# Where the second network enters a fused attention and two-network kernel, and how its weight conversions are ranked

## The chip, the cores and the metric

One core of a Trainium2 chip. The metric is device time of one execution in microseconds (us); lower is better. The engines are named as in the profile: PE (TensorE, matmuls), DVE (VectorE), ACT (ScalarE), POOL (GpSimd) and SP (SyncE, which here only issues transfers).

## The reference

Channel attention over 6016 tokens of 256 channels, then two feed-forward networks, token by token:

```python
qn = q / (norm(q, axis=tokens) + 1e-6);  kn = k / (norm(k, axis=tokens) + 1e-6)
a = softmax(kn.T @ qn / tau)                      # 256 x 256
x = v @ a
h = x @ w_in                                      # first network, 2048 wide
g = where(h >= 1, h, where(h <= -1, 0, (h + 1)**2 / 4))
x = g @ w_out
xn = x / sqrt(mean(x*x, axis=-1) + 1e-6) * rms_g  # second network, 1536 wide
s = xn @ w_gate
out = (s * sigmoid(s) * (xn @ w_val)) @ w_out2
```

All weights come as 64-bit floats, q, k and v as 32-bit.

## The kernel before

**Tiles.** The tokens are cut into 12 tiles t of 512 (the last has 384). Each product is done with operands split into a high and a low part of a matmul type of lower precision (hi by an ACT copy, lo by a DVE subtraction, `split`), and three matmuls per product: high-high, high-low, low-high. A **block** ("1", t, f) of the first network is 128 of the 2048 inner columns: `emit_A`, six matmuls into a PSUM tile h (line L555); `start_g`, two ACT passes and one DVE pass that make g (L564 to L566), the last of which frees the PSUM tile; `finish_g`, the split into gh and gl; and `emit_B`, six matmuls into y (L587), BLAG = 3 blocks later. A block ("2", t, f) of the second network is 128 of 1536 columns: twelve matmuls into gp and vp (L658), Silu and a product (L668, L669), a split into uh and ul, and two such blocks later `emit_D`, six matmuls into the output o (L702; L692 for the last tile).

**Between the networks.** `norm(t)` copies y out of PSUM into an SBUF tile x, makes the sum of squares sa, splits it into sh and sl, adds over partitions by two matmuls into ms (L615, L616), takes a power on POOL, scales x and splits it into xh and xl. It is a generator: each `work(1)` runs it to its next `yield`. `prep_v` does the like for the next tile of v (transposed into vt, split into vh and vl).

**Weights.** The attention matrix is multiplied into w_in once, in four pieces (`product_a`, into w1_ps, evicted into w1h and w1l). Each 64-bit weight piece is loaded into a tile `wide` and made into a high and a low 32-bit part by `narrow`: per piece four or five DVE steps and three or four ACT steps (L203 to L230, and the last subtraction in L120). 34 pieces: eight of w_in, eight of w_out, and 18 of the second network. `pump` advances at most two of them by a step each; `may_W2` holds back the second network's until item W2_FROM of the order.

**The order.** A list `order` of blocks is traced one after the other; behind each, `work` and `pump`. In it the blocks of tiles 0 and 1 are interleaved, then eight blocks of tile 2 (ALONE), then first and second network mixed, 24 blocks of the second remaining at the end. The framework's scheduler then sets each engine's order by its own estimate, by readiness and by rank (traced earlier ranks first); it may split a group of six matmuls. `issue_after(ins)` keeps the traced instructions of an engine behind `ins` on that engine; with `gates` it holds the conversions' steps behind tile 1's last split, until item GATED. `in_order` fixes an engine's order as traced.

**Buffers.** Four PSUM tiles (tag mm) for h, gp, vp, ms and w1_ps in turn, two (yo) for y and o. In SBUF four tmp tiles (g, u, vt, sa, sb and the output tiles ob), three each for gh and gl (sh and sl too), and eight opp tiles (vh, vl, xh, xl).

Of the kernel before, what the change touches and what calls it, by code (L numbers as in the profile page):

```python
# [27 lines left out]
BORROW = (0, 15)  # L28
LENT = 1
# [17 lines left out]
def tile_channel_attention_two_ffn(  # L47
# [270 lines left out]
    jobs += early_jobs[:EARLY]  # L318
    late_wi = early_jobs[EARLY:]

    for at_job, job in zip((0, 3, 4, 7, 8), late_wi):
        later.insert(at_job, job)
    w2 = {}
    for g in range(F2 // TOK):
# [108 lines left out]
        return sub_hi(v_op[t][1][:, c, :], vt[t][c], v_op[t][0][:, c, :])  # L433

    at = []

    def product_a(g):

        h, l = wi.pop(g)
        got = []  # L440
        for b in range(NC):
            ah, al = at[b]
            ps = mm_tile(f"w1_ps{g}_{b}")
            terms = [(ah, w, c) for c in range(NC) for w in (h, l)]
            terms += [(al, h, c) for c in range(NC)]
            for i, (x, w, c) in enumerate(terms):
                nc.tensor.matmul(  # L447
                    ps, x[:, c * P:(c + 1) * P], w[:, c, :],
                    start=(i == 0), stop=(i == len(terms) - 1),
                )  # L450
            got.append(ps)

        def evict(b):
            sl = slice(g * TOK, (g + 1) * TOK)
            hi, lo = w1h[:, b, sl], w1l[:, b, sl]
            nc.scalar.activation(out=hi, in_=got[b], func=AF.Copy, scale=rs[b])
            nc.vector.scalar_tensor_tensor(
                out=lo, in0=got[b], scalar=rs[b], in1=hi.bitcast(F32),
                op0=ALU.mult, op1=ALU.subtract,
            )  # L460

        return evict

# [80 lines left out]
    last_A = [None]  # L544
    g_op = {}
    g_f32 = {}

    def emit_A(t, f):
        _, n = tiles[t]
        vh, vl = v_op[t]  # L550
        ps = mm_tile(f"h{t}_{f}")
        terms = [(w1h, x, c) for c in range(NC) for x in (vh, vl)]
        terms += [(w1l, vh, c) for c in range(NC)]
        for i, (w, x, c) in enumerate(terms):
            last_A[0] = nc.tensor.matmul(  # L555
                ps[:, :n], w[:, c, f * P:(f + 1) * P], x[:, c, :n],
                start=(i == 0), stop=(i == len(terms) - 1),
            )
        return ps

    def start_g(t, f, ps):
        _, n = tiles[t]
        r = tmp_tile(f"g{t}_{f}")
        nc.scalar.activation(out=r[:, :n], in_=ps[:, :n], func=AF.Relu, bias=0.5, scale=0.5)  # L564
        nc.scalar.activation(out=r[:, :n], in_=r[:, :n], func=AF.Square)  # L565
        nc.vector.scalar_tensor_tensor(  # L566
            out=r[:, :n], in0=ps[:, :n], scalar=1.0, in1=r[:, :n], op0=ALU.max, op1=ALU.min
        )
        g_f32[t, f] = r

    def finish_g(t, f):
# [20 lines left out]

    x_op = {}

    def norm(t):
        _, n = tiles[t]
        y = y_ps.pop(t)
        nb = n // 32
        x = big_tile(f"x{t}", "x")
        nc.scalar.activation(out=x[:, 0, :n], in_=y[:, 0, :n], func=AF.Copy)  # L600
        nc.vector.tensor_copy(out=x[:, 1, :n], in_=y[:, 1, :n])
# [14 lines left out]
        nc.tensor.matmul(ps[:, :n], ones_r, sl[:, :n], start=False, stop=True)  # L616
        nc.vector.transpose(out=s1[:, :n], in_=ps[:, :n])
        m = const.tile([P, 16], F32, tag="m", name=f"m{t}")
        nc.gpsimd.tensor_scalar(
# [8 lines left out]
            in_=m[:, :nb].unsqueeze(2).to_broadcast([P, nb, 32]),  # L628
        )
        nc.vector.transpose(out=s1[:, :n], in_=s0[:, :n])  # L630
        for c in range(NC):
# [6 lines left out]
        xl = opp.tile([P, NC, TOK], F32R, tag="op", name=f"xl{t}")  # L638
        for c in range(NC):
            split(xh[:, c, :n], xl[:, c, :n], x[:, c, :n])  # L640
        x_op[t] = (xh, xl)


# [93 lines left out]
    order = [block for _, block in sorted(at_block)]  # L737

    second = [("2", t, f) for t in range(NT) for f in range(NF2)]
    done = 0  # L740
    for t in range(2, NT):
        first = ALONE if t == 2 else 0
        n = NF2 - HELD if t == 2 else NF2 + HELD if t == 3 else NF2
        base = done
        for f in range(NF1):
            order.append(("1", t, f))
            while done < base + n * (f + 1 - first) // (NF1 - first):
                order.append(second[done])
                done += 1
    order += [("B",)] * BLAG  # L750
    order += second[done:]

    tasks = []
    n_norms = [0]
# [12 lines left out]
    def finish_all_g():  # L767
        for key in list(g_f32):
            finish_g(*key)

    def step1(t, f):
        if t == 0 and f in W1_AT:
            make_w1(W1_AT.index(f) + 1)
        ps = emit_A(t, f)
        m1.append((t, f))
        finish_all_g()
        start_g(t, f, ps)
        if len(m1) > BLAG:
            next_B()

    def next_B():
        t, f = m1.pop(0)
        if (t, f) in g_f32:
            finish_all_g()
        if t == 0:
            require(("wo", f // 2))
        emit_B(t, f)
        if f == NF1 - 1:
            n_norms[0] += 1
            tasks.insert(n_norms[0] - 1, norm(t))  # L790

    def step2(t, f):
        if t == 0:
# [14 lines left out]
            store(t)  # L808

    jobs.extend(later)  # L810
    for i, it in enumerate(order):
        if it[0] == "1":
            _, t, f = it
            if t > 0 and f == 0 and t + 1 < NT:
                load_v(t + 1)
            if t > 0 and f == 8 and t + 1 < NT:
                tasks.append(prep_v(t + 1))
            if t == 2 and f >= 8:
                work(1)
            while t not in v_op:  # L820
                work(1)
            step1(t, f)
        elif it[0] == "2":
            while it[1] not in x_op:
                work(1)
            step2(*it[1:])
        else:
            next_B()
        work(1)
        pump()  # L830
        if i % 3 == 0:
            pump()
        if i == GATED:
            gates.clear()
        may_W2[0] |= i >= W2_FROM
    finish_u(*m2[-1])
    did_D(*m2[-2])
    did_D(*m2[-1])
# [35 lines left out]
```

## Time and profile before

| | us |
|---|---|
| median of 3 runs | 1187.37 (1185.89 to 1188.77) |
| the profiled execution | 1187.01 |
| its span in the profile | 1185.1 |
| PE busy | 1161.7 (98%) |
| DVE busy | 664.9 (56%) |
| ACT busy | 648.0 (55%) |
| POOL busy | 68.5 (6%) |

The profiled execution is 1.9 us longer than its span. Busy shares are averages over the span; the slices in [rows 1] are 29.6 us each. The matmuls are pipelined: a matmul of 512 columns is recorded with about 0.39 us, and the next starts about 0.226 us after it, so a busy PE is not PE at its peak, and the number of matmuls in a stretch says more.

### The profile page before, as it was taken

Reading aid. Unit: us, or ns where it says so; the run is one execution under the profiler, and the core shown is the slowest. Engines: PE = TensorE matmul, PEld = TensorE weight load, DVE = VectorE, ACT = ScalarE, POOL = GpSimd, SP = SyncE. Lnnn points to the kernel's source line nnn. Section 1 sums busy time; section 2 is a strip of 40 time slices with the busy share of each in tenths; the row PEclk is TensorE's granted clock in tenths of the full one; section 3 lists DMA queues with packets and bytes.
Section 4 is the critical chain, followed back from the end, with each engine's and each line's share of the span. In section 5 each row is a group of like instructions: output and inputs, shape, how many; then the busy total and the mean of one; then the engine's idle time right before and its main releaser. Section 6 shows DMA issues by size and latency. Waiting matters only on the chain.

```text
span 1185.1 us, 13913 instructions
## 1 busy us (share of the span) xinstructions
PE 1161.7 (98%) x5202; PEld 969.6 (82%) x5202; DVE 664.9 (56%) x1034; ACT 648.0 (55%) x1092; POOL 68.5 (6%) x54
## 2 busy tenths in 40 slices
PE   8889997999999999999999999999999999999998
PEld 6768885888888888888888888888888888888888
DVE  5899999664434644644644643653653654544433
ACT  6689988554445544644644554554555554444332
POOL 0000011010002001001101101100100100100000
PEclk9989998999999999999999999999999999999999
DMA  9923432101101101101010010110100100100110
GB/s 347 248 88 107 124 107 72 18 1 19 18 1 19 19 1 18 17 3 19 1 19 11 8 19 1 19 18 1 18 14 1 19 1 1 19 1 1 19 18 14
DMA packets 107747, 43.36 MB, mean 37 GB/s; under 512 B 97568, under 2 KB 97952, under 8 KB 107680
## 3 DMA queue, kind: packets, MB, share of 16 engines
q1 hardware_dynamic: 107680, 42.48, 14.3%
q8 instruction: 40, 0.66, 0.2%
q14 instruction: 27, 0.22, 0.1%
HBM read 36.31 MB, written 6.16 MB: 36 GB/s over the span
## 4 chain that ended last, share of the span: by engine, by line
PE 90%; DVE 5%; DMA 2%; ACT 1%; issue 1%; SPq 0%; DVEq 0%; ACTq 0%
PE y L587 20%; PE h L555 20%; PE gp L658 16%; PE vp L658 16%; PE o L702 15%; DVE acc L378 1%; PE o L692 1%; PE w_ps L447 1%; DMA qk<-in_k_dram 1%; DMA qk<-in_q_dram 1%; DVE g L566 1%; DVE wide L222 1%; DVE wide L214 1%; DVE gl L120 0%; DMA wide<-in_moe_w_val_dram 0%
## 5 line engine op out<-in xcount | busy, mean ns | idle before, releaser
L566 DVE SCALAR_TENSOR_TENSOR g<-h,g 128x512 f32<-128x512 f32 (+1 forms) x192 | 129.8, 677 | 188.9 <-ACT g L565 188.6
L123 ACT ACTIVATE uh<-u 128x512 fp32r<-128x512 f32 (+1 forms) x144 | 89.8, 624 | 202.2 <-PE o L702 147.1
L564 ACT ACTIVATE g<-h 128x512 f32<-128x512 f32 (+1 forms) x192 | 112.7, 588 | 130.9 <-PE h L555 126.6
L669 DVE TENSOR_TENSOR u<-u,vp 128x512 f32<-128x512 f32 (+1 forms) x144 | 97.2, 675 | 128.8 <-PE vp L658 120.4
L123 ACT ACTIVATE gh<-g 128x512 fp32r<-128x512 f32 (+1 forms) x192 | 118.9, 621 | 82.7 <-DVE g L566 81.2
L555 PE MATMUL h<-vh,w1h 128*128 128x512 f32 (+1 forms) x384 | 149.8, 390 | 3.1 <-DVE g L566 3.1
L555 PE MATMUL h<-vl,w1h 128*128 128x512 f32 (+1 forms) x384 | 149.5, 389 | 0.0
L120 DVE TENSOR_TENSOR gl<-g,gh 128x512 fp32r<-128x512 f32 (+1 forms) x168 | 113.5, 677 | 64.0 <-ACT gh L123 61.3
L587 PE MATMUL y<-gh,woh 128*128 128x512 f32 (+1 forms) x384 | 148.9, 388 | 0.1
L120 DVE TENSOR_TENSOR ul<-u,uh 128x512 fp32r<-128x512 f32 (+1 forms) x144 | 97.6, 677 | 91.4 <-ACT uh L123 91.4
L587 PE MATMUL y<-gh,wol 128*128 128x512 f32 (+1 forms) x384 | 148.3, 386 | 0.0
L565 ACT ACTIVATE g<-g 128x512 f32<-128x512 f32 (+1 forms) x192 | 119.6, 623 | 5.0
L587 PE MATMUL y<-gl,woh 128*128 128x512 f32 (+1 forms) x384 | 118.3, 386 | 0.6 <-DVE gl L120 0.6
L555 PE MATMUL h<-vh,w1l 128*128 128x512 f32 (+1 forms) x384 | 118.5, 389 | 0.0
L668 ACT ACTIVATE u<-gp 128x512 f32<-128x512 f32 (+1 forms) x144 | 84.9, 590 | 49.5 <-PE gp L658 32.4
L658 PE MATMUL gp<-xh,wgh 128*128 128x512 f32 (+1 forms) x288 | 111.0, 385 | 0.0
L658 PE MATMUL vp<-xh,wvh 128*128 128x512 f32 (+1 forms) x288 | 111.0, 385 | 0.0
L658 PE MATMUL gp<-xh,wgl 128*128 128x512 f32 (+1 forms) x288 | 110.9, 385 | 0.0
L658 PE MATMUL vp<-xh,wvl 128*128 128x512 f32 (+1 forms) x288 | 110.8, 385 | 0.0
L702 PE MATMUL o<-uh,wdh 128*128 128x512 f32 x264 | 102.8, 390 | 0.0
L702 PE MATMUL o<-uh,wdl 128*128 128x512 f32 x264 | 102.8, 389 | 0.0
L555 PEld LDWEIGHTS h<-vh,w1h 128*128 128x128 f32 x384 | 72.9, 190 | 19.0 <-DVE g L566 4.4
(121 smaller groups left out, 1751.4 us busy)
## 6 DMA issues: line engine op xcount, KB each, us to landing
wide<-in_moe_w_out_dram SPq DMA_DIRECT2D x14, 512.0 KB, 3.9
vin<-in_v_dram SPq DMA_DIRECT2D x88, 64.0 KB, 2.5
out_dram<-ob SPq DMA_DIRECT2D x88, 64.0 KB, 2.0
qk<-in_q_dram SPq DMA_DIRECT2D x9, 512.0 KB, 10.2
qk<-in_k_dram SPq DMA_DIRECT2D x9, 512.0 KB, 10.2
wide<-in_moe_w_in_dram SPq DMA_DIRECT2D x8, 512.0 KB, 6.9
wide<-in_moe_w_gate_dram SPq DMA_DIRECT2D x6, 512.0 KB, 3.5
wide<-in_moe_w_val_dram SPq DMA_DIRECT2D x6, 512.0 KB, 3.7
```

What stands on the lines that cost most here:

```text
L120: return eng.tensor_tensor(out=dst_lo, in0=src, in1=hi.bitcast(F32), op=ALU.subtract)
L123: nc.scalar.activation(out=dst_hi, in_=src, func=AF.Copy)
L214: nc.vector.scalar_tensor_tensor(out=low, in0=high, scalar=0x80000000, in1=low, op0=ALU.bitwise_and, op1=ALU.bitwise_or,)
L555: last_A[0] = nc.tensor.matmul(ps[:, :n], w[:, c, f * P:(f + 1) * P], x[:, c, :n], start=(i == 0), stop=(i == len(terms) - 1),)
L564: nc.scalar.activation(out=r[:, :n], in_=ps[:, :n], func=AF.Relu, bias=0.5, scale=0.5)
L565: nc.scalar.activation(out=r[:, :n], in_=r[:, :n], func=AF.Square)
L566: nc.vector.scalar_tensor_tensor(out=r[:, :n], in0=ps[:, :n], scalar=1.0, in1=r[:, :n], op0=ALU.max, op1=ALU.min)
L587: nc.tensor.matmul(y_ps[t][:, c, :n], w[:, f, c * P:(c + 1) * P], x[:, :n], start=(f == 0 and w is woh and x is gh), stop=(f == NF1 - 1 an ...
L658: nc.tensor.matmul(ps[:, :n], w[:, c, f * P:(f + 1) * P], x[:, c, :n], start=(i == 0), stop=(i == len(terms) - 1),)
L668: nc.scalar.activation(out=u[:, :n], in_=ps[0][:, :n], func=AF.Silu)
L669: nc.vector.tensor_tensor(out=u[:, :n], in0=u[:, :n], in1=ps[1][:, :n], op=ALU.mult)
L702: nc.tensor.matmul(o_ps[t][:, c, :n], w[:, f, c * P:(c + 1) * P], x[:, :n], start=(f == 0 and w is wdh and x is uh), stop=(f == NF2 - 1 an ...
```

## The change

- The second network's blocks begin 60 blocks behind the first network's beginning (FIRST_ALONE), then 12 for 16; 45 of them remain at the end.
- `take_y` copies y out of PSUM at the next block of the first network, into an opp tile (nine now); `norm` starts 14 items ahead of the tile's first block of the second network, has three yields ahead of its two matmuls for each tile, and three yields more behind them.
- The blocks and the `work` stages are traced in `high_priority`, so the conversions (`pump`) rank behind them. They are held behind the last block's square and DVE pass (`paced`), until item 50.
- The pieces of w_in come in another order, and their products with the attention matrix stand behind items 5, 13 and 21, with the evictions behind the next item.
- From item 32 PE keeps the traced order.

```diff
-PAIR = (1.5, 19.0)
-GATED = 6
-W2_FROM = 28
-ALONE = 8
-HELD = 8
+PAIR = (1.5, 16.5)
+W2_FROM = 20
+FIRST_ALONE = 60
+NORM_LEAD = 14
+PE_FROM = 32
+GATED = 50
+PACE = 1
+AHEAD_OF = 300
 BLAG = 3
-W1_AT = (2, 6, 10)
+W1_AT = (5, 13, 21)
...
-    opp = ctx.enter_context(tc.tile_pool(name="opp", bufs=8))
+    opp = ctx.enter_context(tc.tile_pool(name="opp", bufs=9))
...
-    for at_job, job in zip((0, 3, 4, 7, 8), late_wi):
+    for at_job, job in zip((1, 4, 5, 8, 9), late_wi):
...
     def make_w1(g):
         require(*[("wi", g, c) for c in range(NC)])
-
-        with tc.issue_after(last_A[0].ins):
-            evict = product_a(g)
-        for b in range(NC):
-            evict(b)
+        evict = product_a(g)
+        evicts.extend((evict, b) for b in range(NC))
...
+        if t < 3:
+            paced.append((on_act.ins, on_dve.ins))
         g_f32[t, f] = r
...
-    def norm(t):
+    def take_y(t):
         _, n = tiles[t]
         y = y_ps.pop(t)
-        nb = n // 32
-        x = big_tile(f"x{t}", "x")
+        x = opp.tile([P, NC, TOK], F32, tag="op", name=f"x{t}")
         nc.scalar.activation(out=x[:, 0, :n], in_=y[:, 0, :n], func=AF.Copy)
         nc.vector.tensor_copy(out=x[:, 1, :n], in_=y[:, 1, :n])
-        yield
+        y_sb[t] = x
+
+    def norm(t):
...
+        x = y_sb.pop(t)
...
-        for _ in range(3 if t < 2 else 1):
+        for _ in range(3):
             yield
         ps = mm_tile(f"ms{t}")
...
+    first += [("1", t, f) for t in range(2, NT) for f in range(NF1)]
...
+    for i, block in enumerate(first):
+        order.append(block)
+        while done * NF1 < (i + 1 - FIRST_ALONE) * NF2:
+            order.append(second[done])
+            done += 1
     order += [("B",)] * BLAG
     order += second[done:]
+    norm_at = {max(0, order.index(("2", t, 0)) - NORM_LEAD): t for t in range(NT)}
...
     for i, it in enumerate(order):
+        if i == PE_FROM:
+            ordered.enter_context(in_order(ENG.PE))
+        if i in norm_at:
+            n_norms[0] += 1
+            tasks.insert(n_norms[0] - 1, norm(norm_at[i]))
...
-            step1(t, f)
+            with tc.high_priority(AHEAD_OF):
+                step1(t, f)
+            if i in W1_AT:
+                make_w1(W1_AT.index(i) + 1)
+            else:
+                while evicts:
+                    evict, b = evicts.pop(0)
+                    evict(b)
...
-        work(1)
+        with tc.high_priority(AHEAD_OF):
+            work(1)
         pump()
         if i % 3 == 0:
             pump()
+        if len(paced) > PACE:
+            gates[:] = paced.pop(0)
         if i == GATED:
             gates.clear()
```

What moves, on DVE where the first blocks begin (behind the two splits vl of tile 1; g0_0 is the g of block (0, 0), `wide` a weight piece in conversion). Before:

```order
L120 TENSOR_TENSOR vl1_368<-vt1_1_370,vh1_367 128x512
L203 TENSOR_SCALAR wide_459<-wide_459 128x512
L210 TENSOR_SCALAR wide_459<-wide_459 128x512
L203 TENSOR_SCALAR wide_461<-wide_461 128x512
L210 TENSOR_SCALAR wide_461<-wide_461 128x512
L203 TENSOR_SCALAR wide_467<-wide_467 128x512
L203 TENSOR_SCALAR wide_457<-wide_457 128x512
L214 SCALAR_TENSOR_TENSOR wide_459<-wide_459 128x512
L566 SCALAR_TENSOR_TENSOR g0_0_453<-h0_0_446,g0_0_453 128x512
```

And now:

```order
L123 TENSOR_TENSOR vl1_368<-vt1_1_370,vh1_367 128x512
L206 TENSOR_SCALAR wide_459<-wide_459 128x512
L206 TENSOR_SCALAR wide_457<-wide_457 128x512
L213 TENSOR_SCALAR wide_457<-wide_457 128x512
L217 SCALAR_TENSOR_TENSOR wide_459<-wide_459 128x512
L217 SCALAR_TENSOR_TENSOR wide_457<-wide_457 128x512
L572 SCALAR_TENSOR_TENSOR g0_0_453<-h0_0_446,g0_0_453 128x512
L572 SCALAR_TENSOR_TENSOR g0_1_482<-h0_1_471,g0_1_482 128x512
```

Five conversion steps instead of seven stand ahead of the first g, and the g of block (0, 1) follows it at once.

On DVE where it makes gl of block (2, 8) (sb1, sa1 and sl1 belong to the norm of tile 1; wgl, wvl and wdl are low parts of the second network's weights). Before:

```order
L606 TENSOR_TENSOR sb1_1568<-x1_1554 128x512
L222 SCALAR_TENSOR_TENSOR wide_1929<-wide_1929 128x512
L120 TENSOR_TENSOR wvl_443<-wide_1895,wvh_442 128x512
L566 SCALAR_TENSOR_TENSOR g2_8_1583<-h2_8_1572,g2_8_1583 128x512
L607 TENSOR_TENSOR sa1_1567<-sa1_1567,sb1_1568 128x512
L566 SCALAR_TENSOR_TENSOR g2_9_1610<-h2_9_1599,g2_9_1610 128x512
L120 TENSOR_TENSOR wdl_445<-wide_1929,wdh_444 128x512
L203 TENSOR_SCALAR wide_1997<-wide_1997 128x512
L120 TENSOR_TENSOR sl1_1594<-sa1_1567,sh1_1593 128x512
L120 TENSOR_TENSOR gl2_8_1607<-g2_8_1583,gh2_8_1606 128x512
```

And now:

```order
L225 SCALAR_TENSOR_TENSOR wide_1508<-wide_1508 128x512
L217 SCALAR_TENSOR_TENSOR wide_1515<-wide_1515 128x512
L123 TENSOR_TENSOR gl2_7_1610<-g2_7_1579,gh2_7_1609 128x512
L206 TENSOR_SCALAR wide_1591<-wide_1591 128x512
L572 SCALAR_TENSOR_TENSOR g2_9_1637<-h2_9_1626,g2_9_1637 128x512
L123 TENSOR_TENSOR gl2_8_1634<-g2_8_1613,gh2_8_1633 128x512
L123 TENSOR_TENSOR wdl_445<-wide_1508,wdh_444 128x512
L217 SCALAR_TENSOR_TENSOR wide_1591<-wide_1591 128x512
L225 SCALAR_TENSOR_TENSOR wide_1515<-wide_1515 128x512
L123 TENSOR_TENSOR gl2_9_1657<-g2_9_1637,gh2_9_1656 128x512
```

The norm of tile 1 has left this place, and a conversion step or two stand between one g or gl and the next.

On PE at the first matmul of a norm's sum (ms1 before, ms0 now). Before:

```order
L615 MATMUL ms1_1643<-sh1_1593,ones_r_86 128x512
L555 MATMUL h2_10_1660<-vh2_1027,w1h_82 128x512
L555 MATMUL h2_10_1660<-vl2_1028,w1h_82 128x512
L555 MATMUL h2_10_1660<-vh2_1027,w1h_82 128x512
L555 MATMUL h2_10_1660<-vl2_1028,w1h_82 128x512
L555 MATMUL h2_10_1660<-vh2_1027,w1l_83 128x512 x2
L587 MATMUL y2_1422<-gh2_8_1606,woh_438 128x512
L587 MATMUL y2_1422<-gh2_8_1606,wol_439 128x512
L587 MATMUL y2_1422<-gh2_8_1606,woh_438 128x512
L587 MATMUL y2_1422<-gh2_8_1606,wol_439 128x512
L616 MATMUL ms1_1643<-sl1_1594,ones_r_86 128x512
```

And now:

```order
L595 MATMUL y3_1911<-gh3_0_1858,woh_438 128x512
L595 MATMUL y3_1911<-gh3_0_1858,wol_439 128x512
L595 MATMUL y3_1911<-gl3_0_1859,woh_438 128x512 x2
L629 MATMUL ms0_1918<-sh0_1844,ones_r_86 128x512
L630 MATMUL ms0_1918<-sl0_1845,ones_r_86 128x512
L561 MATMUL h3_4_1921<-vh3_1447,w1h_82 128x512
L561 MATMUL h3_4_1921<-vl3_1448,w1h_82 128x512
```

Before, ten matmuls stand between the two of ms, and a group of y is split by the second; now they follow each other, behind the whole of a block's second product.

## Rows read from the trace of the kernel before

**Rows 1.** The page: busy us, share and instructions; busy tenths in 40 slices; granted clock.

```profile
PE 1161.7 (98%) x5202; PEld 969.6 (82%) x5202; DVE 664.9 (56%) x1034; ACT 648.0 (55%) x1092; POOL 68.5 (6%) x54
...
PE   8889997999999999999999999999999999999998
...
DVE  5899999664434644644644643653653654544433
...
PEclk9989998999999999999999999999999999999999
```

**Rows 2.** Busy time by stretch: from:to, length, each engine busy (starts), PEclk, DMA share, GB/s.

```profile
62.00:67.30 5.30, 1.51 (x6) 0.59 (x4) 5.30 (x12) 5.30 (x11) 0.00 (x0) 0.93 0.22 91
67.30:74.60 7.30, 6.81 (x16) 4.99 (x17) 7.30 (x13) 7.27 (x15) 0.00 (x0) 0.58 0.00 0
74.60:178.00 103.40, 103.27 (x453) 84.63 (x453) 99.99 (x177) 92.02 (x168) 3.22 (x2) 1.00 0.39 112
178.00:192.00 14.00, 12.34 (x51) 8.91 (x49) 14.00 (x26) 13.04 (x25) 0.00 (x0) 1.00 0.39 114
192.00:204.00 12.00, 7.22 (x19) 5.44 (x20) 10.91 (x20) 9.86 (x17) 0.00 (x0) 0.72 0.15 44
57.60:204.00 146.40, 135.55 (x560) 107.69 (x559) 141.66 (x251) 130.84 (x236) 3.22 (x2) 0.95 0.36 104
204.00:300.00 96.00, 96.00 (x425) 79.48 (x424) 55.51 (x86) 49.77 (x84) 7.10 (x4) 1.00 0.07 12
...
300.00:400.00 100.00, 100.00 (x442) 82.81 (x441) 46.41 (x71) 47.59 (x78) 6.97 (x5) 1.00 0.07 11
1000.00:1100.00 100.00, 100.00 (x483) 88.02 (x482) 47.47 (x78) 47.10 (x87) 6.16 (x5) 1.00 0.04 6
```

**Rows 3.** Timeline of PE, 62 to 75 us: start, length, instruction, [idle before it, releaser].

```profile
64.57 0.50 PE L447 MATMUL w_ps<-w1h,ah 128*128 128x512 f32 x1 [1.79 <-DVE g L566]
...
67.31 0.80 PE L555 MATMUL h<-vh,w1h 128*128 128x512 f32 x1 [2.01 <-DVE g L566]
...
74.08 0.72 PE L447 MATMUL w_ps<-w1h,ah 128*128 128x512 f32 x2 [0.49 <-ACT w1h L228]
...
74.64 0.39 PE L587 MATMUL y<-gh,wol 128*128 128x512 f32 x1
```

**Rows 4.** Timeline of PE, 178 to 204 us.

```profile
180.14 0.50 PE L555 MATMUL h<-vh,w1h 128*128 128x512 f32 x1 [1.05 <-DVE g L566]
...
192.08 0.73 PE L587 MATMUL y<-gl,woh 128*128 128x512 f32 x2 [0.59 <-DVE gl L120]
...
197.52 0.79 PE L615 MATMUL ms<-sh,ones_r 128*128 128x512 f32 x1 [4.70 <-ACT sh L123]
...
203.41 0.40 PE L587 MATMUL y<-gh,woh 128*128 128x512 f32 x1
```

**Rows 5.** Timeline of DVE, 59 to 65 us.

```profile
59.82 1.47 DVE L120 TENSOR_TENSOR vl<-vt,vh 128x512 fp32r<-128x512 f32 x2
61.21 0.42 DVE L203 TENSOR_SCALAR wide<-wide 128x512 f32<-128x512 f32 x1
61.54 0.42 DVE L210 TENSOR_SCALAR wide<-wide 128x512 uint32<-128x512 uint32 x1
...
63.23 0.69 DVE L214 SCALAR_TENSOR_TENSOR wide<-wide 128x512 uint32<-128x512 uint32 x1
63.83 0.68 DVE L566 SCALAR_TENSOR_TENSOR g<-h,g 128x512 f32<-128x512 f32 x1
```

**Rows 6.** Instructions by line and shape: busy us, mean ns | idle before them, releasers.

```profile
L566 DVE SCALAR_TENSOR_TENSOR g<-h,g 128x512 f32<-128x512 f32 x176 | 120.8, 688 | 173.0 <-ACT g L565 172.7
L565 ACT ACTIVATE g<-g 128x512 f32<-128x512 f32 x176 | 111.2, 632 | 4.5
...
L564 ACT ACTIVATE g<-h 128x512 f32<-128x512 f32 x176 | 104.9, 597 | 121.0 <-PE h L555 116.8 <-DMA out_dram<-ob 1.4 <-DVE w1l L457 0.9
...
L120 DVE TENSOR_TENSOR ul<-u,uh 128x512 fp32r<-128x512 f32 x132 | 90.9, 689 | 81.7 <-ACT uh L123 81.7
```

More of the change, by code (lines that the diff above doesn't have):

```diff
@@ L435, in tile_channel_attention_two_ffn @@
     at = []
+    w1_made = set()
     def product_a(g):
@@ L460, in evict @@
             )
+            if b == NC - 1:
+                w1_made.add(g)
         return evict
@@ L549, in emit_A @@
         _, n = tiles[t]
+        assert f * P // TOK in w1_made
         vh, vl = v_op[t]
@@ L554, in emit_A @@
         for i, (w, x, c) in enumerate(terms):
-            last_A[0] = nc.tensor.matmul(
+            nc.tensor.matmul(
                 ps[:, :n], w[:, c, f * P:(f + 1) * P], x[:, c, :n],
@@ L564, in start_g @@
         nc.scalar.activation(out=r[:, :n], in_=ps[:, :n], func=AF.Relu, bias=0.5, scale=0.5)
-        nc.scalar.activation(out=r[:, :n], in_=r[:, :n], func=AF.Square)
-        nc.vector.scalar_tensor_tensor(
+        on_act = nc.scalar.activation(out=r[:, :n], in_=r[:, :n], func=AF.Square)
+        on_dve = nc.vector.scalar_tensor_tensor(
             out=r[:, :n], in0=ps[:, :n], scalar=1.0, in1=r[:, :n], op0=ALU.max, op1=ALU.min
         )
+        if t < 3:
+            paced.append((on_act.ins, on_dve.ins))
         g_f32[t, f] = r
@@ L593, in tile_channel_attention_two_ffn @@
     x_op = {}
+    y_sb = {}
+    def take_y(t):
+        _, n = tiles[t]
+        y = y_ps.pop(t)
+        x = opp.tile([P, NC, TOK], F32, tag="op", name=f"x{t}")
+        nc.scalar.activation(out=x[:, 0, :n], in_=y[:, 0, :n], func=AF.Copy)
+        nc.vector.tensor_copy(out=x[:, 1, :n], in_=y[:, 1, :n])
+        y_sb[t] = x
     def norm(t):
         _, n = tiles[t]
-        y = y_ps.pop(t)
         nb = n // 32
-        x = big_tile(f"x{t}", "x")
-        nc.scalar.activation(out=x[:, 0, :n], in_=y[:, 0, :n], func=AF.Copy)
-        nc.vector.tensor_copy(out=x[:, 1, :n], in_=y[:, 1, :n])
-        yield
+        x = y_sb.pop(t)
         s0 = tmp_tile(f"sa{t}")
@@ L630, in norm @@
         nc.vector.transpose(out=s1[:, :n], in_=s0[:, :n])
+        yield
         for c in range(NC):
@@ L736, in tile_channel_attention_two_ffn @@
         at_block.append(((PAIR[0] + f * (PAIR[1] - PAIR[0]) / (NF1 - 1), 1), ("1", 1, f)))
-    order = [block for _, block in sorted(at_block)]
+    first = [block for _, block in sorted(at_block)]
+    first += [("1", t, f) for t in range(2, NT) for f in range(NF1)]
     second = [("2", t, f) for t in range(NT) for f in range(NF2)]
+    order = []
     done = 0
[L741 to L749, printed above, removed]
+    for i, block in enumerate(first):
[3 more added lines that the diff above has]
+            done += 1
     order += [("B",)] * BLAG
     order += second[done:]
+    norm_at = {max(0, order.index(("2", t, 0)) - NORM_LEAD): t for t in range(NT)}
     tasks = []
@@ L769, in finish_all_g @@
             finish_g(*key)
+    done_y = []
     def step1(t, f):
-        if t == 0 and f in W1_AT:
-            make_w1(W1_AT.index(f) + 1)
         ps = emit_A(t, f)
@@ L776, in step1 @@
         finish_all_g()
+        while done_y:
+            take_y(done_y.pop())
         start_g(t, f, ps)
@@ L788, in next_B @@
         if f == NF1 - 1:
-            n_norms[0] += 1
-            tasks.insert(n_norms[0] - 1, norm(t))
+            done_y.append(t)
     def step2(t, f):
@@ L815, in tile_channel_attention_two_ffn @@
                 load_v(t + 1)
-            if t > 0 and f == 8 and t + 1 < NT:
+            if t > 0 and f == (2 if t == 2 else 8) and t + 1 < NT:
                 tasks.append(prep_v(t + 1))
-            if t == 2 and f >= 8:
-                work(1)
             while t not in v_op:
                 work(1)
-            step1(t, f)
+            with tc.high_priority(AHEAD_OF):
[6 more added lines that the diff above has]
+                    evict(b)
         elif it[0] == "2":
@@ L825, in tile_channel_attention_two_ffn @@
                 work(1)
-            step2(*it[1:])
+            with tc.high_priority(AHEAD_OF):
+                step2(*it[1:])
         else:
             next_B()
-        work(1)
+            while done_y:
+                take_y(done_y.pop())
+        with tc.high_priority(AHEAD_OF):
+            work(1)
         pump()
@@ L835, in tile_channel_attention_two_ffn @@
         may_W2[0] |= i >= W2_FROM
+    ordered.close()
     finish_u(*m2[-1])
```

6 lines of the change are left out of this document (5 added, 1 removed).

## The prediction

> **What bounds the kernel now.** I read first the busy shares and the slices [rows 1]: TensorE is busy 98% of the span; apart from the first loads and the last drain, the slices in which it is not, or in which its granted clock falls, lie between the third and the seventh, where VectorE (DVE) stands at nine tenths. Then the busy times by stretch [rows 2]. From 204 us on TensorE has no gap: 425 matmuls in 96.00 us, 442 in 100.00 us, 0.2262 us each, while DVE needs half of the time. So nothing that the change does behind 204 us can win much; it can only lose. From 57.6 us (the first matmul of h) to 204 us TensorE starts 560 matmuls in 146.40 us; at 0.2262 us they need 126.7. The stretch holds **19.7 us of loss**, and DVE is busy 141.66 us of it.
>
> The timeline of TensorE says where the loss lies. [...] Later [rows 4] it waits 1.05 us for L566, 0.59 for a gl, 4.70 for the second tile's sh, and again falls to the lower clock until 203.41 us: 14 matmuls in 5.89 us instead of 3.17, so 2.7 us. Waits 10.6 and clock 5.9 make 16.5; the other 3.2 are gaps below 0.3 us. All these waits end at DVE or at what waits for DVE.
>
> How late DVE is can be counted. It takes 146.40/251 = 0.583 us per instruction, waits included [rows 2]. From its first vl of tile 1 at 59.82 us [rows 5] the sl of the second norm is its 238th instruction: 59.82 + 238 x 0.583 = 198.6 us. On TensorE 553 matmuls stand between 57.6 us and the one that reads it, which without a gap would start at 57.6 + 553 x 0.2262 = 182.7. DVE is 15.9 us behind there, nearly the whole loss. **DVE's instruction count ahead of each matmul is what bounds the stretch.**
>
> **The change at the start.** The last weight conversions and the products of w_in with the attention matrix are reordered. On DVE seven conversion steps stood between vl and the first g; now five stand there, and the second g comes at once (first pair of orders). A TENSOR_SCALAR issues every 0.34 us, the others every 0.60 [rows 5]. So after 61.21 us: 3 x 0.34 + 2 x 0.60 puts the first g at 63.4 to 64.1 and the second at 64.7. TensorE now has four blocks of h (24 matmuls, to 63.0 us) before it needs that buffer: it waits 1.1 us. Two blocks later (66.9) it needs the buffer of h1_0; DVE has 4 x 0.34 + 3 x 0.60 us of conversions ahead of that g, so it ends at 68.4: 1.6 us. Then 0.3 us for the next buffer, and 1.2 for the low half of a converted w_in, which DVE ends at 71.8. Together 4.2 us of waits, where before had 4.3. For the clock the bounds are 0 and the 3.2 us of the same place before. I take 1.5, since part of a slow stretch would fall under the last two waits, when TensorE has nothing ready. Start: 5.7 us, instead of 7.5.
>
> **The change up to 204 us.** The second network now starts 60 blocks of the first network behind its beginning (FIRST_ALONE), so its first matmul stands near 228 us gapless instead of 174.5, and the norms wait until 14 blocks ahead of their use. The weights that it needs may so come later too; the conversions are the same in number. The second pair of orders shows the place. With 0.583 us again: gl of block (2,8) is DVE's 239th instruction before and has 554 matmuls ahead of it; now gl of (2,9) is the 215th with 556 ahead. 59.82 + 215 x 0.583 = 185.2 against 57.6 + 556 x 0.2262 = 183.4: 1.8 us behind instead of 16. Of the instructions before it 16 conversion steps and 13 steps of norms have left, and five others came. Over all blocks from (0,0) to (3,4) I find the largest such lag at (2,1) and (2,4), 3.7 us (DVE 181 and 195 instructions, 460 and 496 matmuls). TensorE is 5.7 us late already from the start, so DVE, the engine that set the end of this stretch, has 2 us to spare. I keep 1.0 us for small gaps, a third of what before has. Loss to 204 us: 4.2 + 1.5 + 1.0 = **6.7 us instead of 19.7, a gain of 13.0**.
>
> **What costs nothing, and its cover.** Copying the raw output out of PSUM at once (take_y) instead of in the norm is the same two copies; 24 to 30 matmuls (5.4 us and more) stand between the last matmul into y and the next that needs its buffer, or the other buffer is used. The raw copies sit in the ninth opp buffer instead of the big x tile. The norm's wait on POOL now has two blocks more of cover. The second network alone at the end grows from 24 to 45 blocks, 18 matmuls (4.07 us) each, with two ScalarE and two DVE instructions of at most 0.69 us [rows 6]; before, that stretch (1000 to 1100 us) has no gap [rows 2]. Transfers: the same DMAs on SP, those of the late weights some us later; the DMA engines are busy 0.07 of the time from 204 us on [rows 2]. The v load of the next tile stands ahead of an out store in SP's queue and waits for DVE's transposes of the tile before; the store behind it is not waited for until its tmp buffer comes round.
>
> **The strict order on TensorE** from block 32 on (in_order) is the unknown. Today the scheduler splits groups of six to slip past waits; now each block stands as written, and a late g or gl stops everything behind it. Where two blocks of the first network stand side by side, 33 places behind block 60, the demand on ScalarE and DVE is closest. A block needs 0.60 + 0.63 + 0.69 us for g [rows 6] and two more such passes for gh and gl, 3.2 us in all; its second product stands 36 matmuls or more (8.1 us) behind its first, and its PSUM buffer comes round after as many. Bounds: 0, and 1.05 us (the wait on L566 in [rows 4]) at each place. I take 0, as 4.9 us of cover remain with both engines half idle [rows 2].
>
> Sum: the profiled execution took 1187.01 us (span 1185.1 and 1.9 around it): 1187.0 - 13.0 = 1174.0. The median of before is 0.36 above that execution, so I forecast **1174.3 us**; from the bounds of the start alone, 1171.5 to 1178.
>
> **Rivals.** A: the wait for the norm comes back at its new place. The first norm's sum of squares now stands behind block (3,0), takes one of the three gh buffers, and two of the four tmp buffers for some nine blocks, in the last blocks in which conversions still run. For it: exactly this wait was the longest before [rows 4]. Against: its sl is DVE's 248th instruction, 204.4 us, against 203.0 for the matmul, 1.4 behind and covered by 5.7. Price as before, 4.70 + 2.7 + 0.6 = 8.0: 1182.
>
> B, the slower side: the strict order waits at each of the 33 places, 33 x 1.05 = 34.7 us: 1209. It decides from 13.0/33 = 0.39 us per place. For it: nothing can go round a late g any more. Against: the cover above. Would the clock then fall too? Before it stays at 1.00 through the 1.05 us wait and through the small gaps from 74.6 to 178 [rows 2, 4]; it fell only with the longer ones. [...]
>
> C: the hold behind each block's activation does more than it says and delays the conversions, until the second network waits for weights. DVE's last conversion step is its 253rd instruction, near 207 us, and the second network's first matmul near 228 + 6.7. For it: the gates are on longer. Against: 27 us of slack. They would have to slip by these and 13 more to eat the gain: 1187.
>
> **Chances.** Forecast 0.76, A 0.13, B 0.08, C 0.03. A change under 0.2% (2.4 us) can't be told from none here. The forecast and A (5 us) are faster: 0.89; C the same: 0.03; B slower: 0.08. The range takes in A and the lower bound of the start: 1170.5 to 1184.
>
> The clock at the start is the least sure term. Before, the lower level came behind the waits of 1.79 and 2.01 us and behind that of 4.70 us, and not behind 1.05 us [rows 3, 4]; now waits of 1.1, 1.6, 0.3 and 1.2 us stand there. [...]
>
> **What would show it.** Right: from about 78 us to the end TensorE has no wait over 0.3 us and a clock of 1.00; DVE is near full to about 205 us; the waits on sh and on gl are gone. Wrong: a wait at ms (A), repeated waits on L572 or a gl behind 230 us (B), a wait of gp for a converted weight (C), or a start as long as before.

## The result and the profile after

The changed kernel took 1174.90 us in its median (1174.24 to 1175.06, 4 runs; the profiled one 1174.88), the kernel before 1187.38 beside it; the ratio is 0.9894, with a 95% interval of 0.9877 to 0.9911. Forecast were 1174.3.

The busy times by stretch, in the columns of [rows 2]:

```profile
57.60:204.00 146.40, 142.31 (x613) 115.38 (x612) 137.30 (x244) 130.73 (x242) 0.00 (x0) 0.99 0.39 109
204.00:300.00 96.00, 95.60 (x421) 78.76 (x420) 55.49 (x87) 59.75 (x102) 8.63 (x7) 1.00 0.04 6
1000.00:1100.00 100.00, 100.00 (x442) 82.57 (x441) 47.77 (x75) 34.48 (x58) 5.59 (x4) 1.00 0.07 11
62.00:67.30 5.30, 3.28 (x9) 2.61 (x10) 5.30 (x12) 5.30 (x11) 0.00 (x0) 0.74 0.22 91
67.30:74.60 7.30, 6.34 (x26) 4.46 (x25) 7.30 (x14) 6.26 (x12) 0.00 (x0) 0.95 0.21 66
192.00:204.00 12.00, 12.00 (x54) 9.95 (x53) 11.85 (x22) 11.97 (x23) 0.00 (x0) 1.00 0.50 131
178.00:204.00 26.00, 26.00 (x116) 21.57 (x115) 24.90 (x44) 25.28 (x48) 0.00 (x0) 1.00 0.44 121
```

From 57.6 to 204 us TensorE now starts 613 matmuls where it started 560 [rows 2]: 53 x 0.2262 = 12.0 us, as much as the spans differ by (1185.1 and 1173.1). Most of it lies where the norm of tile 1 stood: at 178 to 204 us, where TensorE waited 4.70 us for sh and its granted clock fell (0.72 from 192 to 204 us) [rows 2, 4], it starts 116 instead of 51 + 19, and these 46 are 10.4 of the 12.0 us.

The waits of TensorE from 57.6 us to the end (us in total, times, longest):

```profile
PE h L561 <- DVE g L572: 2.2, 1, 2.2
PE w_ps L451 <- DVE w1l L123: 0.9, 1, 0.9
PE y L595 <- DVE gl L123: 0.7, 2, 0.4
PE y L595 <- ACT gh L126: 0.6, 1, 0.6
```

There is none at ms and none on sh. Their places on TensorE's timeline, against [rows 3, 4]:

```profile
64.02 0.50 PE L561 MATMUL h<-vh,w1h 128*128 128x512 f32 x1 [2.24 <-DVE g L572]
...
68.47 0.39 PE L451 MATMUL w_ps<-w1h,ah 128*128 128x512 f32 x1
...
71.71 0.50 PE L451 MATMUL w_ps<-w1l,ah 128*128 128x512 f32 x1 [0.95 <-DVE w1l L123]
```

```profile
166.57 0.50 PE L595 MATMUL y<-gh,woh 128*128 128x512 f32 x1 [0.63 <-ACT gh L126]
...
168.04 0.73 PE L595 MATMUL y<-gl,woh 128*128 128x512 f32 x2 [0.26 <-DVE gl L123]
```

The longest wait stands behind a wait of DVE for a transfer, which the prediction had not seen (DVE's timeline; compare [rows 5]):

```profile
59.62 0.42 DVE L206 TENSOR_SCALAR wide<-wide 128x512 f32<-128x512 f32 x1
61.40 0.43 DVE L206 TENSOR_SCALAR wide<-wide 128x512 f32<-128x512 f32 x1 [1.36 <-DMA wide<-in_moe_w_out_dram]
```

### The profile page after: what moved, and what is told of

Same layout as the page of the kernel before. It is cut to its first block, busy times and chain, and to the rows that moved or that the text cites. A ratio compares the mean times of both kernels' runs of the same rounds, so it can differ in the third digit from the quotient of the medians.

```text
span 1173.1 us, 14011 instructions
## 1 busy us (share of the span) xinstructions
PE 1156.6 (99%) x5202; PEld 966.7 (82%) x5202; DVE 661.6 (56%) x1034; ACT 642.2 (55%) x1092; POOL 69.6 (6%) x54
## 4 chain that ended last, share of the span: by engine, by line
PE 87%; DVE 5%; DMA 3%; ACT 3%; SPq 1%; issue 1%; ACTq 0%; DVEq 0%
PE y L595 18%; PE h L561 18%; PE gp L675 16%; PE vp L675 16%; PE o L719 15%; DVE acc L381 1%; PE o L709 1%; DMA qk<-in_k_dram 1%; DMA wide<-in_moe_w_val_dram 1%; SPq L164 1%; DMA wide<-in_moe_w_out_dram 1%; DVE g L572 1%; ACT g L570 1%; DMA qk<-in_q_dram 1%; ACT gh L126 1%
## 5 line engine op out<-in xcount | busy, mean ns | idle before, releaser
L572 DVE SCALAR_TENSOR_TENSOR g<-h,g 128x512 f32<-128x512 f32 (+1 forms) x192 | 129.9, 677 | 157.3 <-ACT g L571 157.1
L675 PE MATMUL gp<-xl,wgh 128*128 128x512 f32 (+1 forms) x288 | 87.6, 385 | 0.0
```

What stands on the lines that cost most here:

```text
L572: on_dve = nc.vector.scalar_tensor_tensor(out=r[:, :n], in0=ps[:, :n], scalar=1.0, in1=r[:, :n], op0=ALU.max, op1=ALU.min)
L675: nc.tensor.matmul(ps[:, :n], w[:, c, f * P:(f + 1) * P], x[:, c, :n], start=(i == 0), stop=(i == len(terms) - 1),)
```

## The experiments

Theory D is the prediction's: DVE's instruction count ahead of each matmul bounds the stretch to 204 us. Its rivals say that the gain comes from the start (S), or from the strict order (O). Each kernel was timed beside the kernel before, on one chip; the ratios are to that. "+x" below is a median less 0.9894 times the median of the kernel before beside it, that is, less what the changed kernel would take there by its ratio (1173.9 to 1174.8 us). The interval of that ratio makes each "+x" uncertain by about 2 us.

**DVE work added early and late.** The same 18 passes, in two places:

```diff
         split(gh[:, :n], gl[:, :n], r[:, :n], nc.gpsimd if t > 3 and f < 3 else nc.vector)
+        if t == 2 or (t, f) in ((3, 0), (3, 1)):                 # early
+        if (t == 7 and f >= 3) or (t == 8 and 3 <= f < 8):       # late, instead
+            sub_hi(gl[:, :n], r[:, :n], gh[:, :n])
```

Early: 

> The changed kernel with 18 passes more on DVE (gl is written twice, with the same values; 0.60 us each, 10.8 us in all) in the blocks (2,0) to (3,1), while the first network runs alone. Theory D: gl of block (2,14) is DVE's 261st instruction with 616 matmuls ahead of it, a lag of 15.0 us; TensorE is late by some 6.5 us from the start, so 8.5 us are lost: 1183 us, up to 1188 with the lower clock behind the waits. Rival T (TensorE's sum bounds the time and DVE has room): 1175.

Late: 

> The same 18 passes (gl written twice, the same values) in the blocks (7,3) to (8,7), where both networks run side by side and DVE is half idle. Theory D: no lag of DVE ahead of 204 us changes, and a block has 4.9 us of cover: 1174 to 1176 us. Rival W (what counts is DVE's whole work, or a strict order lets any late gl through): the same loss as with the passes in (2,0) to (3,1), 1183 or more.

Early: 1185.60 us (ratio 0.9991, 0.9982 to 1.0000), +11.6, inside the expected span. Late: 1173.67 us (0.9894, 0.9880 to 0.9907), no difference. Below stand the early passes on TensorE's timeline (three of six such waits, 9.5 us in all). Then comes the stretch 550 to 750 us, with the late passes and in the changed kernel: 169 DVE instructions instead of 150, and as many matmuls:

```profile
165.86 0.74 PE L597 MATMUL y<-gl,woh 128*128 128x512 f32 x2 [1.33 <-DVE gl L123]
...
171.94 1.09 PE L597 MATMUL y<-gl,woh 128*128 128x512 f32 x2 [3.02 <-DVE gl L123]
...
187.48 0.74 PE L597 MATMUL y<-gl,woh 128*128 128x512 f32 x2 [2.76 <-DVE gl L123]
```

```profile
550.00:750.00 200.00, 200.00 (x884) 165.51 (x883) 110.81 (x169) 103.76 (x171) 15.34 (x10) 1.00 0.07 11
550.00:750.00 200.00, 200.00 (x884) 165.59 (x883) 99.45 (x150) 102.60 (x171) 15.63 (x11) 1.00 0.07 11
```

The same 10.8 us of DVE work cost some 11.6 us in the one place and nothing in the other. That shows D: it is not DVE's work that counts, but where it stands. The size came out too. From 72 to 225 us TensorE starts 613 matmuls where the changed kernel starts 664, which is 11.5 us. It waits 9.5 us there for gl, and the changed kernel 1.3 us for gl and gh, so 8.2 us are new waits, against the 8.5 that D gave. Behind the wait of 3.02 us the clock fell (0.57 granted from 172 to 176 us): 8 matmuls from 171.94 to 175.39 us took 3.45 us instead of 1.81, so 1.6 us. The other 1.7 us are in neither of the two.

**The hold taken away.**

```diff
-GATED = 50
+GATED = 6
...
-        if len(paced) > PACE:
-            gates[:] = paced.pop(0)
```

> The changed kernel without the hold: no weight conversion step waits for a block's activation (the list of gates stays empty). The conversion steps then come earlier in DVE's order: gl of block (2,1) is DVE's 199th instruction instead of the 181st, at the same 460 matmuls. Theory D (DVE's instruction count ahead of each matmul bounds the stretch to 204 us): at 0.583 us per instruction and 0.2262 us per matmul the largest lag grows from 3.7 to 14.2 us; TensorE is about 6.5 us late from the start already, so 7 to 8 us are lost in (2,0) to (2,8), with up to 3 us of lower clock behind the waits: 1181 to 1186 us. Rival S (the gain comes from the start and the clock there alone): 1174 to 1176. Rival O (the strict order on TensorE makes the gain): 1174 to 1176.

1188.12 us (1.0013, 1.0005 to 1.0022), +14.3. S and O had forecast no difference, and both missed; D was 2 us short of it at the least, and had the place wrong. The longest waits of TensorE from 57.6 to 204 us, and two of them on its timeline:

```profile
PE h L561 <- DVE g L572: 6.0, 4, 2.1
PE y L595 <- ACT woh L231: 2.4, 1, 2.4
PE w_ps L451 <- ACT w1h L231: 2.3, 1, 2.3
PE y L595 <- DVE gl L123: 1.1, 1, 1.1
...
```

```profile
123.32 0.50 PE L561 MATMUL h<-vh,w1h 128*128 128x512 f32 x1 [1.81 <-DVE g L572]
...
126.57 0.50 PE L561 MATMUL h<-vh,w1h 128*128 128x512 f32 x1 [1.59 <-DVE g L572]
```

I had counted DVE's instructions ahead of gl. But an early conversion first delays g, which frees the PSUM buffer of h, so the waits on L572 came at 66 to 151 us and not first at 165. From 120 to 160 us TensorE starts 151 matmuls where the changed kernel starts 176, which is 5.7 us. As much, 5.9 us (226 instead of 252), is lost from 57.6 to 120 us, and 4.8 of it before 80 us (54 instead of 75): there TensorE waits for converted weights (w1h until 72.75 us, woh until 75.91), and the clock falls to 0.67 from 72 to 80 us. So a good part of what the hold is worth is a matter of the start, and S falls only in the form that it was given, with a start that does not depend on the hold.

**The old job order.**

```diff
-    for at_job, job in zip((1, 4, 5, 8, 9), late_wi):
+    for at_job, job in zip((0, 3, 4, 7, 8), late_wi):
```

> The changed kernel with the late pieces of w_in at their old places among the conversions (0, 3, 4, 7, 8 instead of 1, 4, 5, 8, 9). On DVE three conversion steps instead of six stand between the last vl and the first g; the other waits at the start move by a few steps. The largest lag to 204 us is 4.5 us at (0,2), where now the start itself is behind. Theory D: the start loses 5 to 7.5 us either way: 1173 to 1176.5 us. Rival S (the gain comes from the order of the conversions at the start): 1178 or more.

1179.95 us (0.9936, 0.9924 to 0.9948), +5.2. That is a miss for D: the time lies in the span of S, so some 5 us depend on this order. The first product of y now waits for the first converted piece of w_out, and the clock falls a second time (the first time from 54 to 58 us, at 0.60 and 0.55 granted). The last two rows are 69 to 79 us, here and in the changed kernel:

```profile
69.89 0.50 PE L595 MATMUL y<-gh,woh 128*128 128x512 f32 x1 [2.75 <-ACT woh L231]
...
72.49 0.79 PE L595 MATMUL y<-gh,woh 128*128 128x512 f32 x1 [0.85 <-ACT gh L126]
```

```profile
69.00:79.00 10.00, 8.23 (x22) 5.92 (x23) 10.00 (x19) 8.40 (x17) 0.00 (x0) 0.66 0.27 71
69.00:79.00 10.00, 9.04 (x39) 6.85 (x38) 10.00 (x18) 8.52 (x15) 0.00 (x0) 1.00 0.25 81
```

22 matmuls in 10 us instead of 39 are 3.8 us; 87 instead of 95 from 79 to 100 us, where TensorE waits 0.87 us for a g, are 1.8 more. The order of the conversions matters by which weight is done first, which a count ahead of g and gl does not hold.

**The strict order and the ranks.** Three kernels: the changed one without the strict order; without the strict order and without the ranks; and the kernel before with the strict order alone (from block 32 on, by the lines that the change has for it).

```diff
-PE_FROM = 32
+PE_FROM = 10 ** 6
...
-            with tc.high_priority(AHEAD_OF):      # second kernel only, at its three places
+            with ExitStack():
```

Strict order taken away: 

> The changed kernel without the strict order on TensorE: the scheduler may split the groups of matmuls from block 32 on as in the kernel before; all else as it is. Theory D: the largest lag of DVE is 3.0 us instead of 3.7, both below what TensorE is late from the start, so no difference: 1174 to 1176 us, and the small gaps of 200 to 300 us may go (up to 0.8 us). Rival O (the strict order makes the gain, because split groups cost TensorE time or call for DVE's results sooner): 5 us or more lost, 1180 to 1187. Rival B of the prediction turned round (the strict order costs something at its 33 places): up to 3 us won, 1172.

Both: 

> The changed kernel without the strict order on TensorE and without the ranks (the blocks are no longer recorded with a higher priority than the conversions). Without the strict order but with the ranks it took 1189.13 us, with a wait of 1.48 us of TensorE on L685 once per tile behind 340 us. Rival R (the ranks are what makes the scheduler split the groups of six, and the strict order only takes that back): without both, TensorE's order differs from the changed kernel's in 461 rows instead of 3422, and DVE's in 143; the waits at L685 go: 1174 to 1177 us. Rival O (a free order costs these waits whenever the second network starts 60 blocks behind, ranks or not): 1186 to 1190.

Strict order alone, before: 

> The kernel before with one part of the change alone, the strict order on TensorE from block 32 on. Rival O (the strict order makes the gain): 1174 to 1180. Theory D: DVE's orders stay as they were, and in the strict order the sum of squares of the second norm stands at 537 matmuls instead of 553 with the same 238 DVE instructions ahead of its sl, so TensorE is 3 us later there: 1187 to 1192 us, and up to 20 more if, as with the second network at 48, a wait of 1 to 2 us per tile comes in behind 204 us.

They took 1189.13 us (1.0023, 1.0014 to 1.0032), 1172.44 (0.9886, 0.9873 to 0.9900) and 1186.97 (1.0009, 1.0000 to 1.0018). The first is a miss for D, which had forecast no difference: without the strict order but ranked, the kernel loses 15.3 us, all of it behind 340 us. Below are TensorE's longest waits behind 220 us, one of them on its timeline, and ScalarE just before it:

```profile
PE h L561 <- ACT u L685: 8.9, 6, 1.5
PE o L719 <- ACT g L571: 1.5, 1, 1.5
PE o L719 <- DVE ob L731: 1.5, 1, 1.5
...
```

```profile
345.09 0.50 PE L561 MATMUL h<-vh,w1h 128*128 128x512 f32 x1 [1.48 <-ACT u L685]
```

```profile
340.92 0.63 ACT L126 ACTIVATE uh<-u 128x512 fp32r<-128x512 f32 x1 [9.81 <-PE o L719]
```

The scheduler mixed the matmuls of o among those of y, so o lets go of its operands late, ScalarE stands 9.81 us for them, and what it does next, u and the release of a PSUM buffer, comes late for h. D saw none of that: to 204 us DVE's lags are smaller there than in the changed kernel, and behind 204 us D looks at none. With the ranks gone as well, the waits go too, and the time is 1.6 us below the span that R gave. So the ranks make a free order bad, and the strict order takes that back; by the times, having both and having neither can't be told apart. The strict order without the ranks was not run. O falls by the third run: the strict order alone gains nothing in the kernel before.

The traces do show what the strict order costs. TensorE at 160 to 175 us in the changed kernel, and without strict order and ranks:

```profile
160.00:175.00 15.00, 14.11 (x62) 11.00 (x61) 15.00 (x28) 14.46 (x28) 0.00 (x0) 1.00 0.40 100
160.00:175.00 15.00, 15.00 (x68) 12.40 (x67) 14.18 (x26) 14.31 (x27) 0.00 (x0) 1.00 0.33 96
```

Six matmuls are 1.4 us. The run that gives up the strict order and keeps the ranks starts 68 there as well. Neither of the two has a wait listed between 120 and 220 us; the changed kernel has 0.63, 0.26 and 0.40.

**The second network at 48.** Three kernels: at 48; at 48 with v prepared from block 2; at 48 without strict order and ranks (as above).

```diff
-FIRST_ALONE = 60
+FIRST_ALONE = 48
...
-            if t > 0 and f == (2 if t == 2 else 8) and t + 1 < NT:    # second kernel only
+            if t > 0 and f == 2 and t + 1 < NT:
```

At 48: 

> The changed kernel with the second network 48 instead of 60 blocks behind the first (with it the first norm, 14 blocks ahead of its use). Theory D: eleven to twelve DVE instructions of norms and of late conversions come ahead of gl of block (2,7), the 223rd with 534 matmuls ahead of it, a lag of 11.4 us; beyond the 6.5 us that TensorE is late already this is 5 us, with 0 to 3 us of lower clock: 1179 to 1183 us. Rival S (start alone): 1174 to 1176. Rival O (strict order): 1174 to 1176.

With v sooner: 

> The second network at 48, as in the run that took 1208.1 us, with one thing more: every tile's v is prepared from block 2 of the tile before instead of from block 8 (at 60 too it is block 2 for tile 3 alone). At 48 the norm's steps stand ahead of the last vl in the list of tasks, and vl comes on DVE directly ahead of the g of its first block; now it comes 50 DVE instructions sooner. Theory P (behind 211 us the loss is vl's lateness in a strict order): it lost some 23 us there, of which the waits on L632 (0.8 per tile, 9 of them) stay: 1189 to 1195 us. Rival N (the norm's place does it, not vl): 1203 to 1208.

Without strict order and ranks: 

> The second network at 48, v prepared as late as in the run that took 1208.1 us (vl stands directly ahead of the same g on DVE), but without the strict order and without the ranks: 18 other matmuls now go between the first half of the next tile's first block and its second. Theory P (a late vl costs only because nothing may go round it): the waits on vl and L632 are gone; DVE's largest lag ahead of 204 us is 8.7 us, 2 more than TensorE is late already: 1175 to 1181 us. Rival Q (TensorE needs that vl or that buffer anyhow, in any order): 1195 or more.

They took 1208.10 us (1.0183, 1.0169 to 1.0196), 1191.04 (1.0035, 1.0022 to 1.0048) and 1184.43 (0.9973, 0.9963 to 0.9983). The first is a large miss: +34 instead of the 5 to 9 of D. TensorE's waits behind 220 us and one window, at 48:

```profile
PE h L561 <- DVE sb L632: 6.5, 8, 0.8
PE vp L675 <- ACT u L685: 2.1, 8, 0.3
PE h L561 <- DVE vl L123: 2.1, 7, 0.3
```

```profile
400.00:600.00 200.00, 196.76 (x857) 159.96 (x856) 96.63 (x147) 99.67 (x166) 15.26 (x11) 1.00 0.09 14
```

857 matmuls instead of 884 in 200 us are 6.1 us, or 3 us in each tile; about half of it stands in the waits listed. With v prepared sooner the same window is full, and no wait is left behind 220 us:

```profile
400.00:600.00 200.00, 200.00 (x884) 165.57 (x883) 99.09 (x149) 102.24 (x170) 17.07 (x12) 1.00 0.07 11
```

So behind 225 us it is theory P: at 48 the norm's steps fall in the blocks where v is prepared, and v comes last. In a strict order nothing goes round it; without strict order and ranks, and with v as late, no wait is left behind 220 us either. The waits on L632 went with the late v, where I had expected them to stay. This is the prediction's rival B at another distance, with its waits once in each tile. Some three waits of 0.3 to 0.8 us in each tile left the granted clock at 1.00 in the row at 48.

Ahead of 211 us all three lose more than D gives. The third shows it without the strict order:

```profile
177.35 0.80 PE L629 MATMUL ms<-sh,ones_r 128*128 128x512 f32 x1 [2.51 <-ACT sh L126]
...
188.31 0.50 PE L561 MATMUL h<-vh,w1h 128*128 128x512 f32 x1 [1.58 <-DVE g L572]
```

That is rival A, the wait for the norm, in a kernel that takes +9.7 us where D gave at most 6; Q, with 1195 or more, falls. The wait for sh is 2.51 us of it. How much of the rest is the lower clock (0.92 granted from 160 to 204 us there) and how much ScalarE, which no count holds, stays open.

**The transfer that DVE waits for.** The list wide_dma holds the loads of such weight pieces, in the order in which they are traced.

```diff
+            wide_dma.append(nc.sync.dma_start(
...
-                load_v(t + 1)
+                with ExitStack() as behind:
+                    if t == 1:
+                        behind.enter_context(tc.issue_after(wide_dma[0].ins))   # first piece of w_out
+                    load_v(t + 1)
```

> The changed kernel with two DMA issues moved in SP's queue: the first piece of w_out and the next of w_in are issued ahead of the eight loads of the third v tile instead of behind them. The orders of TensorE, DVE and ScalarE are the changed kernel's, instruction for instruction. In the changed kernel the eight issues take 9.2 us of SP's time, and DVE waits 1.36 us at 61.4 us for that piece. Theory D with the prediction's start term: that wait goes, the first g comes 1.4 us sooner, TensorE's wait of 2.24 us at 64.0 falls to about 0.9, and with it some of the 2 us that it runs at the lower clock behind: 1171.5 to 1173.7 us. Rival K (the clock falls all the same, or a later wait takes up what was won): 1174 to 1175. Rival V (the third v tile, some 1 us later, holds DVE's transposes and loses it again): 1175 to 1177.

1173.25 us (0.9890, 0.9876 to 0.9903). By its number it lies in D's span; by its ratio it can't be told from the changed kernel. In its profile the clock fell at another place, though. The changed kernel's windows, then this one's:

```profile
52.00:57.60 5.60, 5.11 (x23) 3.88 (x24) 4.69 (x12) 3.25 (x7) 0.00 (x0) 1.00 0.87 149
57.60:64.00 6.40, 4.18 (x19) 3.13 (x17) 4.91 (x11) 5.38 (x12) 0.00 (x0) 1.00 0.80 256
64.00:68.50 4.50, 4.48 (x13) 3.46 (x14) 4.50 (x10) 4.50 (x10) 0.00 (x0) 0.62 0.00 0
```

```profile
52.00:57.60 5.60, 5.30 (x18) 4.09 (x19) 3.62 (x11) 2.35 (x7) 0.00 (x0) 0.70 1.03 296
57.60:64.00 6.40, 5.62 (x24) 4.14 (x23) 6.27 (x12) 5.32 (x11) 0.00 (x0) 1.00 0.56 127
64.00:68.50 4.50, 3.17 (x14) 2.25 (x14) 4.50 (x10) 4.50 (x10) 0.00 (x0) 1.00 0.00 1
```

And the same two waits on its timeline (its line numbers are two higher):

```profile
63.73 0.50 PE L563 MATMUL h<-vh,w1h 128*128 128x512 f32 x1 [0.78 <-DVE g L574]
...
71.41 0.50 PE L453 MATMUL w_ps<-w1l,ah 128*128 128x512 f32 x1 [0.82 <-DVE w1l L123]
```

Here TensorE was slow behind its idle time at 50 to 52 us; DVE, which waits for its products, was late itself and met no wait for a transfer. In the changed kernel's profile TensorE came 1.2 us sooner (first h at 56.02 us, here at 57.18), DVE then stood 1.36 us for the transfer, and the clock fell at 64 us. Both reach the converted w_in within 0.3 us of each other (71.71 and 71.41). The run without the strict order, whose transfers are as in the changed kernel, says the same: low clock first (0.74 granted from 52 to 54 us, 0.50 from 54 to 56), no wait for the transfer, that matmul at 71.74 us. So this run cannot price the wait of 1.36 us, and K is not excluded.

**All together.** The second network at 60, hold and late norms kept, no strict order, no ranks, that piece first.

> The version that the runs point to: the second network at 60, the hold and the late norms as in the changed kernel, no strict order and no ranks, and the first piece of w_out issued ahead of the third v tile. Theory D: the lags are 3.0 us at most, the waits of 0.6 and 0.3 us at 166 to 168 us and the gap of 0.4 at 207 us go, DVE doesn't wait for that piece: 1171 to 1173.5 us. Rival: the start is set by DVE's chain from the attention matrix on, and nothing more than the 1172.44 us of the run without strict order and ranks comes of it: no difference from that run.

1172.52 us (0.9881, 0.9866 to 0.9895), which is 14.8 us ahead of the kernel before. Its interval overlaps that of the changed kernel and that of the run without order and ranks (1172.44 us), so it can't be told from either. In its profile the clock stays at 1.00 ahead of h, as in the changed kernel's, and DVE waits for no transfer: the first wait on a g is 0.78 us and ends at 62.80 us, instead of 2.24 and 64.02. But the clock then falls later, to 0.50 from 70 to 72 us, so this does not price the transfer either.

## Why the prediction was right

**The bound and the loss to 204 us.** Right, and shown by the passes added early and late. Forecast were 6.7 us of loss; from 57.6 to 204 us it is 146.40 - 613 x 0.2262 = 7.7. That the norm had to leave its place fits as well: at 178 to 204 us lie 10.4 us of the gain, and at 48, where norms come back into the stretch, the three kernels start 32 to 51 matmuls fewer than the changed one from 72 to 204 us (574), which is 7.2 to 11.5 us. The place of the largest lag was right, the gl of (2,1) with 460 matmuls ahead: 461 start from 56.0 to 168.0 us, and there stand the only waits between 72 and 204 us, 0.63 and 0.26 us. But the 2 us to spare were none at that place. TensorE was 4.9 us late from waits and clock, and that gl, due at 59.82 + 181 x 0.583 = 165.3 us, was read at 168.04. The count is good to some 2 or 3 us, and it leaves out ScalarE, whose gh was the longer of the two waits. The sign "no wait over 0.3 us" behind 78 us failed by these 0.63 us, and by one of 0.40 at 206.86.

**The start.** Its sum was nearly right (5.7 us forecast, 4.9 measured), its terms were not. Waits of 1.1 + 1.6 + 0.3 + 1.2 us were forecast, and 2.24 + 0.95 measured. The first was mis-sized by the transfer; the second fell beneath the low clock (0.62 granted from 64.00 to 68.50 us), as the prediction allowed. What it calls the lower level is 0.50 granted in the traces, from 68 to 72 us before and from 66 to 68 us in the changed kernel. For the clock 1.5 us were forecast, between 0 and 3.2; the 3.2 follow from [rows 2, 3], as the 7.33 us from 67.31 to 74.64, less the wait of 0.49 and 16 x 0.2262. In the changed kernel, 12 matmuls from 64.02 to 68.47 us took 4.45 us instead of 2.71, so 1.7. Where the clock fell ahead of h instead, the forecast waits do come: without the strict order, but with the same start, they are 0.78, 1.33 and 0.80 us, and the clock stays at 1.00 from 58 to 80 us. In all seven profiles that keep the changed kernel's job order, hold and ranks, the wait for the converted w_in ends at 71.3 to 72.3 us, whichever engine was slow first. This fits a start that DVE's chain sets; no run here tested that by itself.

**Ahead and behind.** Two terms were not forecast. TensorE reached h 1.6 us sooner (56.02 instead of 57.61 us), since the clock had not fallen ahead of it (1.00 granted from 52 to 57.60 us, 0.70 before). That is luck and not the change: the kernel before with the strict order added, which has the same matmuls up to h, reached it at 56.20. Behind, 204 to 300 us lost 0.9 us, with 421 matmuls instead of 425 and the wait of 0.40 us. The two nearly cancel.

**The strict order.** It was costed at nothing. By the times no cost can be measured; by the traces it is some 1.4 us at 160 to 175 us. The reason given, that DVE and ScalarE are half idle, was too weak: at 48 they are as idle (DVE 96.63 of 200 us) and 3 us go per tile. And the prediction did not ask what the order prevents: with the ranks in place, 15 us.

**The parts.** Taken out one at a time, the hold is worth 14 us, the distance of 60 instead of 48 some 34 with the strict order and 10 without, the job order 5. They don't add up to 12.5, since each was taken out of a kernel fitted to the others. The early copy of y with its ninth buffer, the places of the products with the attention matrix, PAIR and W2_FROM were not taken out by themselves, so what they are worth is not shown.

**Rivals.** A and B did not come, but both came at 48. C did not come either: the hold gains 14 us.

## What to carry to other kernels

Where one engine follows another, count the follower's instructions ahead of each matmul that needs it, for every result that is waited for (the one that frees a buffer too), and compare with how late the matmul is anyway. Here 10.8 us of DVE work in such a place cost some 11.6 us, 1.6 of them by the clock (0.57 granted for 4 us behind a wait of 3.02 us); elsewhere the same work cost nothing that could be measured. Take parts that answer to each other, such as a rank and a fixed order, out together as well as singly. In a fixed order a change of distance also moves what falls beside what; look at the last step ahead of each tile's first block.

## What the runs showed of the hardware

TensorE stood 2.4 us at 50 to 52 us in the changed kernel, with the late passes and with the piece first, behind the same matmuls. The granted clock stayed at 1.00 behind it in the first two profiles, and was 0.52 to 0.62 from 52 to 56 us in the third. The kernel before shows both as well: 0.70 from 52 to 57.6 us in its own profile, with 16 matmuls, and 1.00 with the strict order added, with 22. Where the clock had fallen there, with the piece first, it stayed up through the waits of 0.78 and 1.33 us behind; where it had not, in the changed kernel, it fell behind the wait of 2.24 us (0.62 from 64.00 to 68.50 us). It fell both times in the kernel before, the second time with the waits of [rows 3] (0.58 from 67.30 to 74.60 us); both times under the old job order, the second time with the wait of 2.75 us (0.66 from 69 to 79 us); and both times without strict order and ranks (0.50 from 54 to 56 us, and from 72 to 74), there the second time behind waits of no more than 0.78, 1.31 and 0.57 us. What decides it at that point is not settled by these runs.
